# A transformer block's backward pass on one core: layer norm split over the first chunks, more buffers for the dK/dV stores, smaller loads in the first late stage

## The chip, the cores and the metric

The kernel runs on one core of a Trainium2 chip. The metric is the device time of one execution in microseconds (us), taken as the median of repeated runs. A core has TensorE (PE: matmuls; its weight loads, PEld, overlap them), VectorE (DVE), ScalarE (ACT), GpSimd (POOL) and SyncE (SP). In this kernel SP and POOL do little but issue DMAs, in the order in which the program gives them, and a DMA that has to wait holds up those behind it on the same queue. Matmul results lie in PSUM, everything else in SBUF or in the device's DRAM.

## The reference: what is computed

One block's output and the gradients of all inputs but one. x is 2048 x 576, there are 32 heads of width 128 with 2048 cached keys and values each, and the gated feed-forward part is 4608 wide; everything is bf16.

```python
xn = layernorm(x)
q = heads(xn @ wq); p = softmax(q @ k.T * 128 ** -0.5)
s = concat(p @ v) @ wo
h = sigmoid(xn @ w_gate) * (xn @ w_up)
out = x + s * silu(h @ w_down)
# returned: out, and by vjp(grad_out): dx, dk, dv, dwq, dwo, dw_gate, dw_up, dw_down
```

## The kernel before, in words

x is held as 16 row tiles of 128 rows (NT = 16). The work runs in stages.

**The first stage (L300 to L455)** loads x, `w_gate` and `w_up`, normalizes x, turns it (a transpose on PE through PSUM) into `xnT`, and computes the gate and up products. The 4608 columns are nine chunks of 512 in five groups: chunk 0 alone, then four groups of two (`groups1`). For every group, all row tiles are passed; for each chunk PE does five matmuls into `g_ps` (L418) and five into `u_ps` (L420), ACT takes the sigmoid (L425), DVE the product (L426), and POOL stores both (L439, L440). Both PSUM tiles have three buffers. The layer norm of a tile is: `bn` (statistics on DVE, L349 and L350), `rstd` for several tiles at once (a square root on ACT, L355, which needs another activation table than the sigmoid; then two short DVE operations), `norm` (ACT, L363), `turn` (five PE transposes, L369, into one of two `pt` buffers) and `put_T` (the copy into `xnT`, by the helper at L40). Tiles 0 and 1 are done first, tiles 2 and 3 and the statistics of tiles 4 to 6 ahead of the loop. All the rest is done within the 16 row tiles of chunk 0: the nine `bn` of tiles 7 to 15 in the first few, two or three per row, then one `rstd` for all nine; `norm` runs three tiles ahead of the row, `turn` two ahead. All weights are loaded through SP, after tiles 0 to 6 of x; tiles 7 to 15 follow the first chunk of both weights. From the second group on, a guard (`guard_step`) loads the key cache and `wq` in pieces through SP into the memory of x and sums their squares on ACT and DVE in turn, spread evenly over the chunk steps; before that, x is stored to DRAM (`xn_d`, L446).

**A second stage** (L503) computes the down product and the elementwise gradients.

**Attention (from L565)** is written as slots: a head has 32 slots, 16 for `main1` (scores by L600, exponentials by L618) and 16 for `main2` (`dp` by L670; then, for one half of the row, ACT L677 and DVE L678, and for the other DVE L673). Other work is put into slots by `plan`, with the slot number written out; b1 and b2 are a head's first slots of the two kinds. `main1` and `main2` send each row tile through a DMA transpose on SP (`PT`, `dST`, L594), and five slots later `tail1` and `tail2` (L647) multiply with it. dV and dK are summed in two halves of the query tiles (`Partial`): the first half goes to `part`, the second is added to it on DVE (L718) into a tile `kvo` and stored by POOL (L720), in four pieces of four blocks for each output. `kvo` comes from the pool `stg`, with two buffers. The second half of dV lies in slots b2 to b2+7, that of dK in b2+16 to b2+23, which are the next head's first slots. `scale_qn` (L636) scales a tile of Q for dK; `scale_don` does it for dV. The key and value loads of the next head (L178) are put into slots too.

**The late stages (from L825)**: the first one (L869 to L917) multiplies each row tile's attention output by `wo`. Its input `oT` is read from DRAM by a DMA transpose on SP (L554), two tiles ahead, into three places that attention has left (in `KQ`, `xnT` and `xn_all`). PE does 64 matmuls (L902) for a tile. DVE then needs `dsg`, `g2b` and `xb`, which `group_loads` loads through POOL (L876) for two tiles at a time, one group ahead, with two buffers; the output tile is stored from `xb` (L912). The next stages compute the weight gradients (L932, L985) and dx (L1103).

In the first late stage and after it, SP and POOL keep the order of the program, as they do in the first stage.

Of the kernel before, what the change touches and what calls it, by code (L numbers as in the profile page):

```python
# [9 lines left out]
bf = mybir.dt.bfloat16  # L10
f32 = mybir.dt.float32
PSUM = bass.MemoryType.PSUM
DRAM = bass.MemoryType.DRAM
P = 128
# [52 lines left out]
def kernel(  # L67
# [164 lines left out]
    with tc.tile_pool(name="pa", bufs=1) as pa:  # L232
# [75 lines left out]
        with tc.tile_pool(name="a1w", bufs=1) as wp:  # L308
# [5 lines left out]
                    for w_ in (wg_sb, wu_sb):  # L314
                        eng.memset(w_[:LO, DT - 1, c0:c1], 0.0)

            def load_w(w_, src, c0, c1):
                nf = DT - 1 if KPAD else DT
                if nf:
                    nc.sync.dma_start(w_[:, :nf, c0:c1], src[:nf * P, c0:c1].rearrange("(i p) c -> p i c", p=P))  # L320
                if KPAD:
                    nc.sync.dma_start(w_[LO:, nf, c0:c1], src[nf * P:, c0:c1])

            XF = min(7, NT)
            for xs, xe in ((0, 1), (1, 2), (2, XF)):
                if xs < xe:
                    nc.sync.dma_start(x_all[:, xs:xe, :], x2[xs * P:xe * P, :].rearrange("(t p) d -> p t d", p=P))
            zero_cols(nc.vector, 0, FCH)
            zero_cols(nc.gpsimd, FCH, F)
            for gi, (fa, fz) in enumerate(groups1):  # L330
                load_w(wg_sb, B_w_gate, fa * FCH, fz * FCH)
                load_w(wu_sb, B_w_up, fa * FCH, fz * FCH)
                if gi == 0 and NT > XF:
                    nc.sync.dma_start(x_all[:, XF:, :], x2[XF * P:, :].rearrange("(t p) d -> p t d", p=P))
            FMAX = nc.vector.BN_STATS_FMAX
            nchunk = 1
            while D % nchunk != 0 or D // nchunk > FMAX:
# [1 line left out]
            with tc.tile_pool(name="a0", bufs=3) as sb0, tc.tile_pool(name="a0ps", bufs=2, space=PSUM) as ps0, \  # L339
# [21 lines left out]
                def norm(st):  # L361
                    xt = x_all[:, st, :]
                    nc.scalar.activation(xt, xt, AF.Identity, bias=nbias[:, st:st + 1], scale=rstd_all[:, st:st + 1])  # L363

                def turn(st):
                    pts[st] = ps0.tile([P, 8, P], bf, name="pt", tag="tr")
                    for i in range(DT):
                        c0 = min(i * P, D - P)
                        nc.tensor.transpose(pts[st][:, i, :], x_all[:, st, c0:c0 + P], ident[:])  # L369

                def put_T(st, eng):
                    alt.copy(xnT[:, :, st * P:(st + 1) * P], pts.pop(st)[:, :DT, :], eng=eng)

                LA = min(2, NT)
                L1 = min(7, NT)
                for st in range(LA):
                    bn(st)
                rstd(0, LA)
# [4 lines left out]
                for a, b in ((LA, min(LA + 2, L1)), (min(LA + 2, L1), L1)):  # L383
# [4 lines left out]
                    if a == LA:  # L388
                        for st in range(a, b):
                            norm(st)  # L390
                bn_left = list(range(L1, NT))
                wd_left = list(range(0, FT, 3))

                def load_wd():
# [1 line left out]
                    f1 = min(f0 + 3, FT)  # L396
                    nc.gpsimd.dma_start(wd_sb[:, f0:f1, :], B_w_down[f0 * P:f1 * P, :].rearrange("(t p) d -> p t d", p=P))

                nstep = sum(NT * (fz - fa) for fa, fz in groups1[1:])
                ntot = len(pieces) + GLA  # L400
                step = 0
                for gi, (fa, fz) in enumerate(groups1):
                    for st in range(NT):
                        if gi == 0:
                            if LA + 2 <= st + LA + 1 < NT:
                                norm(st + LA + 1)
                            if st and st + LA < NT:
                                turn(st + LA)
                        srows = slice(st * P, (st + 1) * P)
                        a_row = rows.tile([P, NB2F * FCH], bf, name="a_row")  # L410
                        h_row = rows.tile([P, NB2F * FCH], bf, name="h_row")
                        for fc in range(fa, fz):
                            fs = slice(fc * FCH, (fc + 1) * FCH)
                            cs = slice((fc - fa) * FCH, (fc - fa + 1) * FCH)
                            g_ps = ps.tile([P, FCH], f32, name="g_ps")
                            u_ps = ps.tile([P, FCH], f32, name="u_ps")
                            for i, (d0, kd) in enumerate(dts):
                                nc.tensor.matmul(g_ps[:], lhsT=xnT[:, i, srows], rhs=wg_sb[:, i, fs], start=(i == 0), stop=(i == DT - 1))  # L418
                            for i, (d0, kd) in enumerate(dts):
                                nc.tensor.matmul(u_ps[:], lhsT=xnT[:, i, srows], rhs=wu_sb[:, i, fs], start=(i == 0), stop=(i == DT - 1))  # L420
                            if gi == 0 and st + LA < NT:
                                if st == 0:
                                    turn(LA)
                                put_T(st + LA, "s")
                            nc.scalar.activation(a_row[:, cs], g_ps[:], AF.Sigmoid)  # L425
                            nc.vector.tensor_tensor(h_row[:, cs], u_ps[:], a_row[:, cs], op=ALU.mult)  # L426
                            if gi:
                                step += 1
                                while gk[0] < min(ntot, ntot * step // max(1, nstep - 14)):
                                    guard_step()  # L430
                                    if gk[0] == ntot:
                                        guard_reduce()
                            elif bn_left:
                                for _ in range(min(3 if st == 0 else 2, len(bn_left))):
                                    bn(bn_left.pop(0))
                                if not bn_left:
                                    rstd(L1, NT)
                        nn = (fz - fa) * FCH
                        nc.gpsimd.dma_start(h_d[srows, fa * FCH:fz * FCH], h_row[:, :nn])  # L439
                        nc.gpsimd.dma_start(a_d[srows, fa * FCH:fz * FCH], a_row[:, :nn])  # L440
                        if gi > 1 and st % 2 and wd_left:
                            load_wd()
                    if gi == 0:
                        for t0 in range(0, NT, 4):
                            t1 = min(t0 + 4, NT)
                            nc.gpsimd.dma_start(xn_d[t0 * P:t1 * P, :].rearrange("(t p) d -> p t d", p=P), x_all[:, t0:t1, :])  # L446
                while gk[0] < ntot:
                    guard_step()
                    if gk[0] == ntot:
# [112 lines left out]
    def attention(fast):  # L562
        with ExitStack() as es:
# [126 lines left out]
            class Partial:  # L690
# [9 lines left out]
                def step(self):  # L700
                    kt = self.kt
                    j = kt % 4
                    if j == 0:
                        self.tile = acc_tile()
                    for qt in range(self.lo, self.hi):
                        nc.tensor.matmul(self.tile[:, j, :], lhsT=self.slabs[qt][:, kt * P:(kt + 1) * P], rhs=self.rhs[:, qt, :],  # L706
                                         start=(qt == self.lo), stop=(qt == self.hi - 1))
                    self.kt += 1
                    if j == 3 or self.kt == NT:
                        k0 = kt - j  # L710
                        if self.out_dram is None:
                            if self.factor == 1.0:
                                alt.copy(self.part[:, k0:kt + 1, :], self.tile[:, :j + 1, :], eng=self.eng)
                            else:
                                alt.scaled(self.part[:, k0:kt + 1, :], self.tile[:, :j + 1, :], self.factor, eng=self.eng)
                        else:
                            fo_ = stg.tile([P, 4, P], bf, name="kvo")
                            nc.vector.scalar_tensor_tensor(fo_[:, :j + 1, :], self.tile[:, :j + 1, :], self.factor, self.part[:, k0:kt + 1, :],  # L718
                                                           op0=ALU.mult, op1=ALU.add)
                            nc.gpsimd.dma_start(self.out_dram.rearrange("(p t) d -> p t d", t=NT)[:, k0:kt + 1, :], fo_[:, :j + 1, :])  # L720
# [30 lines left out]
            def plan(h):  # L751
# [22 lines left out]
                put(b1 + q(NSC + 2), NT * P, lambda: prep_vt(hd()))  # L774
                put(b1 + q(NTH + 2), NT * P, lambda: prep_qn(hd()))
                for qt in range(NT):
                    put(max(b1 + qt + 1, b1 + NT - 4 + qt // 2), 0, lambda qt=qt: scale_qn(hd(), qt))
                put(b2 + 1, 0, lambda: post1(hd()))
                parts = {}

# [54 lines left out]
    with late("pc") as pc, late("pcw") as pcw, late("pcf") as pcf, \  # L835
# [21 lines left out]
                if i == DT - 1 and KPAD:  # L857
                    nc.gpsimd.memset(wdT_sb[:LO, i, r0:r0 + WCH], 0.0)

        with late("c1l3", 2) as ldp3, late("c1s", 2) as sb, \  # L860
                late("c1ps", 2, space=PSUM) as ps, late("c1pt", 2, space=PSUM) as pst:
            wo_of = {}
            for view, h0, n, _ in wo_parts:
# [2 lines left out]
            oTs.append(oT_view(xn_all[:].rearrange("p t d -> p (t d)"), 0))  # L866
            if NT > 2:
                load_oT(oTs[2], 2)
            SG1 = ldiv(NT, 2)  # L869
            NG1 = NT // SG1  # L870

            def group_loads(g):
# [4 lines left out]
                    res.append(t_)  # L877
                return res

            groups = {0: group_loads(0)}  # L880
            pend_tr = []
            for st in range(NT):
                if st and st + 2 < NT:
                    load_oT(oTs[(st + 2) % 3], st + 2)
                g, sl = divmod(st, SG1)
                if sl == 0:
                    if g + 1 < NG1:
                        groups[g + 1] = group_loads(g + 1)
                    dsg, g2b, xb = groups.pop(g)
                if st >= NT - 2 - DT and len(wd_pieces) > (F // WCH - 1) * DT:  # L890
                    wd_piece()
# [285 lines left out]
```

## Time and profile before

| what | value |
|---|---|
| median of 14 runs | 5087.19 us (5064.58 to 5099.43) |
| the profiled execution's own time | 5106.43 us |
| its span, first to last instruction | 5104.4 us |
| mean granted clock of PE | 0.992 |
| PE busy, first stage's rows after chunk 0 (43 to 335.5 us) | 291.69 of 292.50 us |
| PE busy, start (8.87 to 43 us) | 27.43 of 34.13 us |
| PE busy, first tiles of the first late stage (3690 to 3728 us) | 22.18 of 38.00 us |
| PE busy, the rest of it (3728 to 3850 us) | 112.97 of 122.00 us |

How to read it: the profile is of one execution. A group's row gives the line, the engine, the operation, the tiles (out<-in), and then the busy time, the mean ns of one, and the idle time of the engine before it with what ended it. In the waits, "X <- Y: a, b, c" says that X's engine stood idle for Y, a us in total, b times, at most c us. In a timeline a row begins with start and duration in us, merges neighbours of one kind (x16), and ends with the idle time before it in brackets. The granted clock is the share of TensorE's full clock in a stretch. The DMA share is the mean busy share of the 16 DMA engines and can exceed 1 where packets overlap.

### The profile page before, as it was taken

How to read it: one execution, taken by the hardware profiler on the slowest of the kernel's cores; microseconds unless marked ns; L12 is line 12 of the kernel's file. 1: busy time of each engine (PE TensorE's matmuls, PEld its weight loads, DVE VectorE, ACT ScalarE, POOL GpSimd, SP SyncE). 2: the span in 40 equal slices, each digit the busy share in tenths (PEclk: the TensorE clock that was granted, in tenths of full speed). 3: DMA queues.
4: the chain of work that ended last, by engine and by line, in shares of the span. 5: the costliest groups of instructions: out<-in, count | busy, mean ns of one | idle time of the engine just before them, and what ended most of it. 6: DMA issues, size and time to landing. Idle time of an engine off the chain costs nothing.

```text
span 5104.4 us, 128938 instructions
## 1 busy us (share of the span) xinstructions
PE 4984.7 (98%) x54480; PEld 3486.7 (68%) x54480; DVE 2582.3 (51%) x6705; ACT 2574.9 (50%) x4636; POOL 938.9 (18%) x1449
## 2 busy tenths in 40 slices
PE   8999999999999999999999999999889999999999
PEld 4445777777777777777777777777645666555554
DVE  4544666666566666656656665666424444200111
ACT  5422666666666676666666666666413333211000
POOL 3322111111111111111111111111112222211000
PEclk9999999999999999999999999999999999999999
DMA  8777999999999999999999999999996665797986
GB/s 267 261 200 171 199 201 206 203 209 211 204 202 213 205 211 207 202 210 208 213 191 200 203 212 206 208 203 206 210 186 190 188 188 184 221 261 187 174 141 121
DMA packets 2762161, 1031.37 MB, mean 202 GB/s; under 512 B 2664737, under 2 KB 2668962, under 8 KB 2761570
## 3 DMA queue, kind: packets, MB, share of 16 engines
q1 hardware_dynamic: 2660354, 699.97, 74.9%
q0 software_dynamic: 101216, 323.05, 20.0%
q8 instruction: 428, 7.01, 0.6%
q14 instruction: 163, 1.34, 0.1%
HBM read 175.31 MB, written 182.13 MB: 70 GB/s over the span
## 4 chain that ended last, share of the span: by engine, by line
PE 85%; issue 7%; DMA 5%; DVE 2%; POOL 1%; ACT 1%; POOLq 0%; SPq 0%; DVEq 0%; ACTq 0%
PE acc L706 15%; PE acc L647 14%; PE acc L932 13%; PE sp L600 8%; PE acc L1103 7%; PE dp L670 7%; PE acc L213 5%; PE g_ps L418 3%; PE u_ps L420 3%; PE dh L985 3%; PE acc L503 2%; PE acct L146 2%; DMA out_dram<-kvo 2%; PE acc L902 2%; DMA KQ<-on_d 1%
## 5 line engine op out<-in xcount | busy, mean ns | idle before, releaser
L618 ACT ACTIVATE Pq<-sp 128x1024 bf16<-128x1024 f32 x1024 | 1047.0, 1023 | 319.6 <-PE sp L600 307.4
L706 PEld LDWEIGHTS <-Pq 128*128 128x128 bf16 x16384 | 1005.7, 98 | 242.9 <-issue 5.4
L677 ACT ACTIVATE t<-dp,negdelta 128x1024 bf16<-128x1024 f32 x512 | 571.1, 1116 | 222.7 <-PE dp L670 210.1
L673 DVE SCALAR_TENSOR_TENSOR Pq<-dp,negdelta,Pq 128x1024 bf16<-128x1024 f32 x512 | 655.1, 1279 | 43.8 <-PE dp L670 42.8
L670 PE MATMUL dp<-VT,dOT 128*128 128x512 bf16 x2048 | 614.4, 382 | 42.7 <-DVE Pq L673 42.7
L600 PE MATMUL sp<-KQ 128*128 128x512 bf16 x2048 | 609.9, 380 | 2.6 <-ACT Pq L618 2.4
L647 PEld LDWEIGHTS <-PT 128*128 128x128 bf16 x8192 | 502.6, 98 | 132.6 <-DMA PT<-Pq 11.9
L647 PE MATMUL acc<-Kn,dST 128*128 128x128 bf16 x8192 | 551.3, 219 | 6.5 <-DMA dST<-Pq 6.2
L647 PE MATMUL acc<-Vn,PT 128*128 128x128 bf16 x8192 | 547.8, 219 | 10.0 <-DMA PT<-Pq 9.9
L706 PE MATMUL acc<-dOn,Pq 128*128 128x128 bf16 x8192 | 547.0, 219 | 0.0
L706 PE MATMUL acc<-Qn,Pq 128*128 128x128 bf16 x8192 | 543.4, 220 | 0.0
L647 PEld LDWEIGHTS <-dST 128*128 128x128 bf16 x8192 | 491.9, 98 | 69.6 <-DMA dST<-Pq 8.8
L678 DVE TENSOR_TENSOR Pq<-t,Pq 128x1024 bf16<-128x1024 bf16 x512 | 354.2, 692 | 360.1 <-ACT t L677 353.4
L687 ACT ACTIVATE dq_n<-acc,rsc 128x128 bf16<-128x128 f32 x512 | 188.1, 367 | 340.3 <-PE acc L647 339.2
L1119 DVE SCALAR_TENSOR_TENSOR junk<-acc,xn_all 128x512 f32<-128x512 f32 (+1 forms) x32 | 13.9, 452 | 638.0 <-ACT dxn L1118 638.0
L720 POOL DMA_DIRECT2D out_dram<-kvo x256 | 140.3, 548 | 1067.5 <-DVE kvo L718 1067.5
L641 POOL DMA_DIRECT2D on_d<-o_n x128 | 97.0, 758 | 744.7 <-DVE junk L659 390.8
L987 DVE TENSOR_TENSOR du_blk<-dh,ah 128x256 bf16<-128x256 f32 x288 | 120.0, 417 | 194.5 <-PE dh L985 192.5
L718 DVE SCALAR_TENSOR_TENSOR kvo<-acc,part 128x512 bf16<-128x512 f32 x256 | 175.9, 687 | 78.4 <-DMA out_dram<-kvo 44.7
L670 PEld LDWEIGHTS <-dOT 128*128 128x128 bf16 x2048 | 164.1, 98 | 70.5 <-issue 48.3
L1118 ACT ACTIVATE dxn<-acc 128x512 f32<-128x512 f32 (+1 forms) x32 | 12.8, 406 | 394.9 <-PE acc L1103 387.4
L50 DVE TENSOR_SCALAR o_n<-acc,rinv_all 128x128 bf16<-128x128 f32 x352 | 123.2, 350 | 169.8 <-PE acc L647 169.8
(206 smaller groups left out, 6914.2 us busy)
## 6 DMA issues: line engine op xcount, KB each, us to landing
out_dram<-kvo POOLq DMA_DIRECT2D x256, 128.0 KB, 4.2
ah<-a_d POOLq DMA_DIRECT2D x18, 1024.0 KB, 7.1
ah<-h_d POOLq DMA_DIRECT2D x18, 1024.0 KB, 9.3
du_d<-du_blk POOLq DMA_DIRECT2D x18, 1024.0 KB, 8.0
dg_d<-dg_blk POOLq DMA_DIRECT2D x18, 1024.0 KB, 9.7
h_d<-h_row POOLq DMA_DIRECT2D x64, 256.0 KB, 3.4
x_all<-in_A_k_cache_dram SPq DMA_DIRECT2D x64, 256.0 KB, 3.9
a_d<-a_row POOLq DMA_DIRECT2D x64, 256.0 KB, 3.7
```

Source lines behind the costliest of these rows:

```text
L213: nc.tensor.matmul(av[:, :CH], lhsT=w[:, i, :], rhs=srcT[:, i, cs], start=(i == 0), stop=(i == DT - 1))
L600: nc.tensor.matmul(sp[:, c * CH:(c + 1) * CH], lhsT=hs.QT[:, qt * P:(qt + 1) * P], rhs=hs.KT[:, hf * HW_ + c * CH: hf * HW_ + (c + 1) * CH ...
L618: nc.scalar.activation(Pq[:, hsl], sp[:], AF.Exp, scale=SCALE, accum_out=hs.rsp[:, hf:hf + 1])
L647: nc.tensor.matmul(hs.acc[:, 0, :], lhsT=T[:, kt, :], rhs=rhs[:, kt, :], start=(kt == 0), stop=(kt == NT - 1))
L670: nc.tensor.matmul(dp[:, c * CH:(c + 1) * CH], lhsT=hs.dOT[:, qt * P:(qt + 1) * P], rhs=hs.VT[:, hf * HW_ + c * CH: hf * HW_ + (c + 1) * C ...
L673: nc.vector.scalar_tensor_tensor(Pq[:, hsl], dp[:], hs.negdelta[:, qt:qt + 1], Pq[:, hsl], op0=ALU.add, op1=ALU.mult)
L677: nc.scalar.activation(t[:], dp[:], AF.Identity, bias=hs.negdelta[:, qt:qt + 1], scale=1.0)
L678: nc.vector.tensor_tensor(Pq[:, hsl], t[:], Pq[:, hsl], op=ALU.mult)
L687: nc.scalar.activation(hs.dq_n[:, qt % G4, :], hs.acc[:, 0, :], AF.Copy, scale=hs.rsc[:, qt:qt + 1])
L706: nc.tensor.matmul(self.tile[:, j, :], lhsT=self.slabs[qt][:, kt * P:(kt + 1) * P], rhs=self.rhs[:, qt, :], start=(qt == self.lo), stop=(q ...
L932: nc.tensor.matmul(accs[j][:, :nn], lhsT=lhs[:, st, cols], rhs=rhs[:, st, n0:n0 + nn], start=(st == 0), stop=(st == NT - 1))
L1103: nc.tensor.matmul(self.accs[sl][j][:, :nn], lhsT=ch[:, kk, sl * P:(sl + 1) * P], rhs=wT[:, k0 + kk, n0:n0 + nn], start=(self.k + kk == 0) ...
```

## The change

Three parts.

1. *Attention.* `kvo` gets four buffers. `scale_qn` of tiles 8 to 15 moves from slots b2 to b2+3 (two per slot) to b2+8 to b2+15 (one per slot).
2. *First stage.* The order of loads becomes x tiles 0 and 1, gate chunk 0 (SP) and up chunk 0 (on ACT's queue), x tiles 2 to 6, x tiles 7 to 15, the other weights. The loop passes chunk 0 and the first group of two chunks for tiles 0 to 6, then both for tiles 7 to 15, then the other groups for all tiles. `norm` of tiles 4 to 6 is issued from the first row on; `bn` of tiles 7 to 15 one per chunk step while tiles 0 to 6 are at chunks 1 and 2, then `rstd` and one `norm` per step; a `turn` follows as soon as its `norm` has been issued. The `xn_d` stores and the guard's first steps come after the last of these.
3. *First late stage.* The loads are for one tile at a time, two tiles ahead, with four buffers; the output is stored tile by tile.

```diff
-            XF = min(7, NT)
-            for xs, xe in ((0, 1), (1, 2), (2, XF)):
...
+            for st in range(LA):
+                load_x(st, st + 1)
             zero_cols(nc.vector, 0, FCH)
             zero_cols(nc.gpsimd, FCH, F)
...
+            load_w(wg_sb, B_w_gate, 0, FCH)
+            load_w(wu_sb, B_w_up, 0, FCH, nc.scalar)
+            load_x(LA, L1)
+            load_x(L1, NT)
+            for fa, fz in groups1[1:]:
...
+                todo = {"norm": list(range(min(LA + 2, L1), L1)), "turn": list(range(LA, L1)), "bn": list(range(L1, NT))}
+
+                def ln_step(first):
+                    if first or not todo["bn"]:
+                        if todo["norm"]:
+                            norm(todo["norm"].pop(0))
+                        return
+                    bn(todo["bn"].pop(0))
+                    if not todo["bn"]:
+                        rstd(L1, NT)
+                        todo["norm"] = list(range(L1, NT))
+                        todo["turn"] = list(range(L1, NT))
+                        norm(todo["norm"].pop(0))
+
+                def turn_step():
+                    if todo["turn"] and not (todo["norm"] and todo["norm"][0] <= todo["turn"][0]):
+                        st = todo["turn"].pop(0)
+                        turn(st)
+                        return st
...
+                rows_order = [(gi, st) for half in ((0, L1), (L1, NT)) for gi in range(min(2, gi_max)) for st in range(*half)]
+                rows_order += [(gi, st) for gi in range(2, gi_max) for st in range(NT)]
...
+                        ready = None
+                        if n_row:
+                            ready = turn_step()
+                        if gi == 0 and st < L1 and todo["norm"]:
+                            ln_step(True)
...
+                        if not n_row:
+                            ready = turn_step()
+                        if ready is not None:
+                            put_T(ready, "s")
                         nc.scalar.activation(a_row[:, cs], g_ps[:], AF.Sigmoid)
                         nc.vector.tensor_tensor(h_row[:, cs], u_ps[:], a_row[:, cs], op=ALU.mult)
+                        if gi or st >= L1:
+                            if todo["bn"] or todo["norm"]:
+                                ln_step(False)
...
+                        if begin is not None:
+                            while gk[0] < min(ntot, ntot * (step - begin) // max(1, nsteps - 14 - begin)):
...
-                            fo_ = stg.tile([P, 4, P], bf, name="kvo")
+                            fo_ = stg.tile([P, 4, P], bf, name="kvo", bufs=4)
...
-                    put(max(b1 + qt + 1, b1 + NT - 4 + qt // 2), 0, lambda qt=qt: scale_qn(hd(), qt))
+                    put(max(b1 + qt + 1, b1 + NT - 4 + qt // 2 if qt < NTH else b1 + NT + qt), 0, lambda qt=qt: scale_qn(hd(), qt))
...
-        with late("c1l3", 2) as ldp3, late("c1s", 2) as sb, \
+        with late("c1l3", 4) as ldp3, late("c1s", 2) as sb, \
...
-            SG1 = ldiv(NT, 2)
+            SG1 = 1
...
-            groups = {0: group_loads(0)}
+            groups = {g: group_loads(g) for g in range(min(2, NG1))}
...
-                    if g + 1 < NG1:
-                        groups[g + 1] = group_loads(g + 1)
+                    if g + 2 < NG1:
+                        groups[g + 2] = group_loads(g + 2)
```

## The prediction

> **What bounds the kernel now.** I read the page first, then TensorE's waits, then the stretches where those waits lie.
>
> ```profile
> span 5104.4 us, 128938 instructions
> ...
> PE 4984.7 (98%) x54480; PEld 3486.7 (68%) x54480; DVE 2582.3 (51%) x6705; ACT 2574.9 (50%) x4636; POOL 938.9 (18%) x1449
> ```
>
> PE is busy 98%, so 5104.4 - 4984.7 = 119.7 us of idle time, and whatever PE does at less than full clock, is all that an edit off PE can win. The change takes no matmul away. TensorE's waits:
>
> ```profile
> PE dp L670 <- DVE Pq L673: 42.7, 46, 5.4
> PE acc L902 <- DMA KQ<-on_d: 24.4, 2, 16.7
> PE pt L369 <- ACT x_all L363: 13.3, 3, 6.6
> ```
>
> (us in total, times, longest.) Three causes, and each lies in one of the three places that the diff touches. First attention: one head, in the timeline.
>
> ```profile
> 2625.00 1.06 PE L706 MATMUL acc<-dOn,Pq 128*128 128x128 bf16 x16
> ...
> 2635.28 0.69 DVE L718 SCALAR_TENSOR_TENSOR kvo<-acc,part 128x512 bf16<-128x512 f32 x1 [5.59 <-DMA out_dram<-kvo]
> 2635.89 1.27 DVE L673 SCALAR_TENSOR_TENSOR Pq<-dp,negdelta,Pq 128x1024 bf16<-128x1024 f32 x1
> ...
> 2637.21 1.01 PE L670 MATMUL dp<-VT,dOT 128*128 128x512 bf16 x2 [3.97 <-DVE Pq L673]
> ...
> 2640.58 1.55 PE L706 MATMUL acc<-Qn,Pq 128*128 128x128 bf16 x16
> ```
>
> DVE stands 5.59 us before the fourth kvo, until the second one's store has landed; L673 is queued behind it and frees the PSUM of dp; PE waits 3.97 us. Afterwards the same sixteen matmuls take 1.55 us, not 1.06: the clock. Two stretches with their granted clock (PE busy, PEld, DVE, ACT, POOL, then clock, DMA share, GB/s):
>
> ```profile
> 2500.00:2600.00 100.00, 99.76 (x1295) 79.36 (x1293) 63.84 (x173) 68.61 (x117) 17.28 (x29) 1.00 1.10 207
> 2634.80:2641.60 6.80, 4.39 (x30) 3.27 (x30) 3.76 (x4) 2.49 (x3) 1.29 (x2) 0.50 1.23 198
> ```
>
> An undisturbed head leaves nothing to win (99.76 of 100; heads are 97.68 us apart there). Last, the start of the first late stage (issues and their time to landing), and the start of the kernel:
>
> ```profile
> dsg<-dsg_d POOLq DMA_DIRECT2D x3, 288.0 KB, 18.9
> ...
> KQ<-on_d SPq DMA_TRANSPOSE x1, 32.8
> ```
> ```profile
> 27.27 1.28 ACT L355 ACT_TABLE_LOAD   x1 [5.50 <-DVE mv_all L350]
> ...
> 30.28 0.71 PE L369 MATMUL pt<-ident,x_all 128*128 128x128 bf16 x5 [5.71 <-ACT x_all L363]
> ```
>
> **Part 1, four kvo buffers.** Removed: DVE's wait on kvo stores, 44.5 us in 16 waits in attention. Each output has four kvo (16 blocks by 4); the next output's follow eight slots later, above 20 us at 2.65 us a slot, and no kvo store took over 11.7 us to land, so four buffers never wait. On the path lies not 44.5 but PE's idle time behind it: the fifteen gaps above 0.3 us before L670 in attention sum to 35.3 us (0.4 to 5.4). After eight of them the clock falls to 0.50 for 3.4 or 6.8 us; half of the busy time in these windows (2.2 us of the 4.39 shown, 1.7 us in a short one) is lost: 2 x 2.2 + 6 x 1.7 = 15 us. Together 50 us.
>
> What is late next? The stores are slow because everything is: in this head the dST transposes issued at 2620.5 and 2623.7 took 11.6 and 12.1 us, against a median of 4.9. tail2 takes its dST five slots after the issue. I moved each tail2 start forward by its stall and set it against its landing: in 15 stalls the dST would be late in five, by 2.5, 0.3, 1.2, 0.2 and 0.3 us (one later one by 0.6): 5 us comes back. So -45 us; bounds -50 (no dST late) and -20 (the burst of transfers merely moves, and dST misses its slack as often as kvo does now).
>
> Moving eight scale_qn per head (L636, 0.246 us each): before, two per slot in slots b2 to b2+3, beside kvo, o_n and junk; now one per slot in b2+8 to b2+15, where DVE has 0.69 + 1.28 + 0.25 = 2.2 us for a slot of 2.65 us. Their reader, dK's second half, begins at b2+16. Hidden; cost 0, and at most 0.25 us a head (8 us) if L673 stood behind each without that slack; gain at most the same.
>
> **Part 2, the layer norm.** Removed: the gap of 5.71 us (all nine bn, 1.0 us each, then the square root with its table load, were due before the tenth tile) and its half clock: 27.0 to 33.8 at 0.50, PE busy 3.52 there, 1.8 us lost. Also the 0.99 us before tile 4's transpose, since norm(4) is now queued ahead of the first Sigmoid's table load. Sum 8.5 us. The nine bn, nine norm (0.86), nine copies (0.69) and the two table loads (1.28) move to chunk steps of 2.16 us, or 2.44 with a transpose: DVE 1.0 + 0.69, ACT 0.60 + 0.86 + 0.69 = 2.15. It fits, without slack on ACT, but PE has three PSUM buffers and turned tiles ahead, so the table loads hide. The xn_d stores (POOL) and the first guard loads (SP) move behind it; the guard's 91 steps then share some 100 chunk steps instead of 114, which ACT (44% busy there) and DVE (48%) take. SP issues the later weights ahead of them as before.
>
> Added: tiles 2 to 6 of x now follow both weight pieces. Before, x2-6 landed at 7.06, wg at 9.02, wu at 10.98. The bytes up to wu are the same, so x2-6 land near 10.9, wg at about 8.4. Before, 3.6 us passed from bn(2)'s start at 7.80 to norm(2)'s end at 11.4; begun at 10.9 it ends at 14.5. turn(2) waits for it behind a first row that now ends near 12.4: 2 us of idle PE. Behind it, ACT runs norm(4), which waits for bn(4..6), ahead of put_T(2) and the first Sigmoid; put_T(2) ends near 19.0, not 14.4, and row 2 starts near 19.3 instead of 17.4. Rows 3 and 4 wait for put_T and for the two buffers of pt. By these steps row 6 starts at about 29.6; it started at 34.7: gain 5. Bounds: +3 (a cold clock through these waits) and -10. I take -4.
>
> The Trainium skill ("DMA: Bandwidth & Descriptors", Rules for kernel authors) says that spreading DMAs over issuing engines brings no bandwidth, since all share the same DMA engines. The row agrees in its way: the DMA share is already 1.05 and more from 3 us on, one queue alone. So wu on ACT's queue gains SP's issue time only (0.66 + 0.77 us) and is paid by x2-6; without the rule I would have put turn(2) 2 us earlier.
>
> **Part 3, the late stage by tiles.** What could go: 16.66 us before the fourth tile's oT, with 2.5 us of half clock after it. Six group loads of 288 KB (1.77 MB) were issued within 4 us, oT's transpose at 3695.98 ran into them and landed after 32.8 us; in the undisturbed stretch an oT lands after 8.3. Now nine loads of 144 KB (1.33 MB) stand there, later three per tile. In the steady part a burst of three 288 KB loads and a store (1.18 MB) does not hold oT up, while 1.77 MB did: 1.33 is nearer to the first. Bounds: -19 and, below nothing, +10 (POOL stood 16.4 us before xb's load, until a store had landed; now nothing holds the loads back, and oT waits as long or longer). Between the ends I take -8. The gap of 7.8 us at 3829 follows from 2 MB of ah loads and wdT transposes: it stays. The last tile's three loads now queue behind the ah loads, +0 to +3 us; I take 0.
>
> Here a rule speaks against the change: the same page's rules advise coalescing into transfers of 1 MiB and more, and its section "Anatomy of one DMA" fits a DMA of POOL's kind with 2.0 us plus bytes / 436 GB/s. By it (an estimate) 24 loads of 288 KB cost 24 x 2.7 = 64 us, and 48 of 144 KB 48 x 2.3 = 112 us: +48 us if they ran singly. The rows: three such loads land 4 to 5 us after their issue, side by side, inside a tile's 8.1 us. POOL issues 24 loads and 8 stores more, 32 x 0.71 = 23 us over 16 tiles, and is mostly idle there. I follow the row: 0.
>
> **Sum.** -45 - 4 - 8 = -57 against the profiled execution's 5106.4 us: 5049. That execution lies 19 us above the median of 14 runs (5087.2); the runs themselves spread over 35 us, which fits stalls that come and go with DMA. If the 19 us were such stalls, the median has fewer to lose and the new median is near 5049; if they are the profiler's, it is 5087 - 57 = 5030. I take the middle: 5039.
>
> **Rivals.**
> A (likeliest, 0.60): as summed; 5012 to 5062.
> B (0.20): the DMA burst in each head stays, and dST waits take kvo's place: 20 us of the 50 are won, nothing in the late stage, 4 at the start: 5087 - 24 = 5063, range 5055 to 5077. For it: transfers take 11 to 12 us there whoever waits; against: dST's slack of five slots held in ten of 15 cases.
> C (0.06): late stage and start win in full (19 + 10) and kvo 50: 5087 - 79 = 5008.
> D (0.06): the x2-6 delay and the late stage's bound cost what kvo's lower bound wins: 5087 - 20 + 3 + 10 = 5080, no measurable change (within 0.2%, 10 us, is about what a measurement of this kernel cannot tell from none).
> E (0.08), slower: unblocked POOL keeps load bursts in flight beside every oT. A tile needs 1.05 MB of oT and 4 x 0.147 of loads and stores, 1.64 MB per 8.12 us, 202 GB/s; undisturbed the stage had 211, the disturbed stretch about 95. If the slow rate lasts, a tile takes 17 us, +9; from six tiles on it eats the 49 us of the other parts, over 13 tiles it is +117: 5087 - 49 + 117 = 5155. Against: before, the loads had the same mean rate, and twelve tiles ran undisturbed.
>
> Range 5010 to 5078. Faster 0.86, same 0.06, slower 0.08.
>
> **What will show it.** No wait of kvo on its store; L670's wait on L673 from 42.7 to below 10 us; clock 1.00 through most of attention; waits of L647 on dST up by some 5 us (B: 20 or more). No idle gap over 3 us at 24 to 31 us, but one of about 2 us before turn(2), and the Sigmoid's first table load later. KQ<-on_d at the late stage's start landing in under 20 us (E: several oT above 20). I am wrong if dST takes over kvo's waits, or if the oT gap stands as it was.

## The result, and the profile after

| | before | after | after / before |
|---|---|---|---|
| median, us | 5079.76 (47 runs, 5054.84 to 5101.96) | 5049.96 (10 runs, 5043.10 to 5058.41) | 0.994 (0.9926 to 0.9955) |
| profiled execution, us | 5106.43 | 5034.82 | 0.986 |

The change makes the kernel 0.6% faster, 30 us by the medians. The prediction was 5039 with a range of 5010 to 5078: the direction and the range held. (5039 was 48 us under the median of 5087.2 that stood at hand then.) The two profiled executions differ by more, 71.6 us: the one of before lies 27 us above its median, the one of after 15 us below. So a row by row comparison of these two profiles alone overstates the change by some 42 us, and the experiments have to show which of the differing rows belong to the change.

Lines have moved: up to 7 further at the start (turn L369 is L376, norm L363 is L370, `rstd` L355 is L362), 28 further from the chunk loop on (L670 is L698, L673 is L701, L718 is L746, L902 is L930).

The page's head for after (PE was 4984.7 of 5104.4 us before):

```profile
span 5033.0 us, 129057 instructions
...
PE 4966.5 (99%) x54480; PEld 3474.5 (69%) x54480; DVE 2580.9 (51%) x6705; ACT 2574.4 (51%) x4636; POOL 950.5 (19%) x1481
```

Idle time of PE fell from 119.7 to 66.5 us, and PE's own busy time by 18.2 us with the same 54480 matmuls: that fits half clock which is gone (mean granted clock 0.992 before, 0.997 after). The waits of PE in after (total us, times, longest):

```profile
PE pt L376 <- ACT x_all L370: 14.7, 10, 8.3
PE acc L675 <- DMA PT<-Pq: 11.4, 4, 5.9
PE dp L698 <- DVE Pq L701: 7.6, 32, 0.2
PE acc L930 <- DMA KQ<-on_d: 5.7, 2, 5.0
PE acc L675 <- DMA dST<-Pq: 3.5, 7, 1.0
```

Read against the three waits of before: `dp` on L673 fell from 42.7 to 7.6 us, and what is left is 32 waits of at most 0.2, one per head. The wait on `dST` did not grow (6.2 before, 3.5 after). The late stage's wait on `KQ` fell from 24.4 to 5.7. The layer norm's wait did not fall at all: 13.3 in three waits before, 14.7 in ten after (6.6 and 8.3 of it are the wait for the first tile).

DVE in one head of after, at the fourth `kvo` of an output, where before DVE stood 5.59 us:

```profile
2605.59 0.69 DVE L706 TENSOR_TENSOR Pq<-t,Pq 128x1024 bf16<-128x1024 bf16 x1 [0.76 <-ACT t L705]
2606.20 0.68 DVE L746 SCALAR_TENSOR_TENSOR kvo<-acc,part 128x512 bf16<-128x512 f32 x1
2606.80 1.27 DVE L701 SCALAR_TENSOR_TENSOR Pq<-dp,negdelta,Pq 128x1024 bf16<-128x1024 f32 x1
```

L746 follows its neighbour without a bracket, and so does L701. The stretch around it (us and busy time of PE, PEld, DVE, ACT, POOL, then clock, DMA share, GB/s):

```profile
2600.00:2700.00 100.00, 99.76 (x1294) 79.42 (x1293) 64.48 (x168) 67.87 (x115) 17.64 (x29) 1.00 1.09 207
```

99.76 of 100 us at full clock is what the prediction showed of an undisturbed head. In after almost all heads are such heads, 97.68 us apart; before, 13 of them were longer by more than 0.5 us, at most by 7.2 us.

At the late stage's start, the issues of after and their median us to landing (stretch 3633 to 3680):

```profile
dsg<-dsg_d POOLq DMA_DIRECT2D x6, 144.0 KB, 8.0
...
KQ<-on_d SPq DMA_TRANSPOSE x2, 21.2
```

Before, the transpose into `KQ` took 32.8 us; now the median of two is 21.2, and PE waits at most 5.0 us for `KQ` rather than 16.7. Whether the smaller loads did that, this pair can't say. The layer norm in after, where the second pass of tiles begins:

```profile
48.89 1.28 ACT L362 ACT_TABLE_LOAD   x1
...
52.81 0.45 PE L376 MATMUL pt<-ident,x_all 128*128 128x128 bf16 x5 [3.50 <-ACT x_all L370]
...
54.71 2.34 PE L448 MATMUL u_ps<-wu_sb,xnT 128*128 128x512 bf16 x5
...
59.96 0.45 PE L376 MATMUL pt<-ident,x_all 128*128 128x128 bf16 x5 [0.41 <-ACT x_all L370]
```

The gap of 5.71 us has become one of 3.50 us at tile 7, with half clock behind it (L448's five matmuls take 2.34 us here and 1.24 at full clock), and then seven gaps of 0.36 to 0.41 us, one for each of tiles 9 to 15.

### The profile page after: what moved, and what is told of

It reads as the page before. It is cut to its first block, busy times and chain, and to the rows that moved or that the text cites. A ratio compares the mean times of both kernels' runs of the same rounds, so it can differ in the third digit from the quotient of the medians.

```text
span 5033.0 us, 129057 instructions
## 1 busy us (share of the span) xinstructions
PE 4966.5 (99%) x54480; PEld 3474.5 (69%) x54480; DVE 2580.9 (51%) x6705; ACT 2574.4 (51%) x4636; POOL 950.5 (19%) x1481
## 4 chain that ended last, share of the span: by engine, by line
PE 90%; DMA 3%; issue 3%; DVE 2%; ACT 1%; POOL 0%; POOLq 0%; SPq 0%; ACTq 0%; DVEq 0%
PE acc L734 17%; PE acc L675 16%; PE acc L960 13%; PE sp L628 9%; PE dp L698 8%; PE acc L1131 7%; PE acc L213 5%; PE g_ps L446 3%; PE u_ps L448 3%; PE dh L1013 3%; PE acc L531 2%; PE acct L146 2%; PE acc L930 2%; DMA dST<-Pq 1%; DMA KQ<-on_d 1%
## 5 line engine op out<-in xcount | busy, mean ns | idle before, releaser
L701 DVE SCALAR_TENSOR_TENSOR Pq<-dp,negdelta,Pq 128x1024 bf16<-128x1024 f32 x512 | 655.0, 1279 | 37.6 <-PE dp L698 37.6
L698 PE MATMUL dp<-VT,dOT 128*128 128x512 bf16 x2048 | 609.9, 379 | 7.6 <-DVE Pq L701 7.6
L675 PEld LDWEIGHTS <-PT 128*128 128x128 bf16 x8192 | 502.4, 98 | 134.3 <-DMA PT<-Pq 13.3
L675 PEld LDWEIGHTS <-dST 128*128 128x128 bf16 x8192 | 492.0, 98 | 66.5 <-DMA dST<-Pq 5.6
L633 DVE TENSOR_REDUCE rs_all<-rsp 128x1 f32<-128x2 f32 x512 | 78.0, 152 | 256.4 <-ACT Pq L646 254.2
L646 ACT ACTIVATION_READ_ACCUMULATOR Pq<-sp 128x1 f32 x1024 | 200.4, 196 | 0.0
```

What stands on the lines that cost most here:

```text
L646: nc.scalar.activation(Pq[:, hsl], sp[:], AF.Exp, scale=SCALE, accum_out=hs.rsp[:, hf:hf + 1])
L675: nc.tensor.matmul(hs.acc[:, 0, :], lhsT=T[:, kt, :], rhs=rhs[:, kt, :], start=(kt == 0), stop=(kt == NT - 1))
L698: nc.tensor.matmul(dp[:, c * CH:(c + 1) * CH], lhsT=hs.dOT[:, qt * P:(qt + 1) * P], rhs=hs.VT[:, hf * HW_ + c * CH: hf * HW_ + (c + 1) * C ...
L701: nc.vector.scalar_tensor_tensor(Pq[:, hsl], dp[:], hs.negdelta[:, qt:qt + 1], Pq[:, hsl], op0=ALU.add, op1=ALU.mult)
```

## The experiments

Two theories for the gain. Theory K: it is all the `kvo` store; the layer norm and the late stage give about nothing, and what the first pair shows in the late stage is chance. Theory S: the three parts each give what the first pair of profiles shows, some 50, -2.5 and 20 us. Below, "stage 2" is the time at which the first matmul of the second stage begins, "attention" goes from the first scores matmul (`sp`, 151.9 us later in every profile) to the late stage's first `oT` matmul, "late" from there to the next stage's first matmul (in us, of each profile). For orientation, the first pair of profiles: before 335.6, 3200.5, 158.3; after 338.2, 3148.6, 137.6.

### Each part alone

**The kernel before, unchanged, beside the others.**

> The kernel before, unchanged, for a second profile. Theory (the profiled execution of before had more stalls than a usual one, its time was 26 us above the median): kvo waits of DVE in sum 20 to 40 us instead of 44.7, in other heads than before, a time of 5065 to 5090 us. Rival (the profiler itself adds the 26 us): again 5100 to 5110 us with kvo waits of about 45 us in the same heads.

Measured (a single run): 5073.62 us; stage 2 at 335.1, attention 3190.9, late 133.2. Its waits of DVE on the store and of PE on L673 and on `KQ`:

```profile
DVE kvo L718 <- DMA out_dram<-kvo: 37.9, 15, 5.3
```
```profile
PE dp L670 <- DVE Pq L673: 38.5, 46, 4.3
...
PE acc L902 <- DMA KQ<-on_d: 1.8, 1, 1.8
```

The store's waits are there again, 37.9 us of them, and, against the expectation, in the same groups of heads (listed below at the ring of eight); the late gap isn't: 1.8 us with nothing changed. The issues at that place (3670 to 3715) show why it could be:

```profile
dsg<-dsg_d POOLq DMA_DIRECT2D x3, 288.0 KB, 4.7
...
KQ<-on_d SPq DMA_TRANSPOSE x2, 13.0
```

With the old loads of 288 KB the transposes landed after 13.0 us (median) in this execution. So the 16.7 us on `KQ` do not come in every execution.

**Part 1 alone.**

```diff
-                            fo_ = stg.tile([P, 4, P], bf, name="kvo")
+                            fo_ = stg.tile([P, 4, P], bf, name="kvo", bufs=4)
```

> The kernel before with four kvo buffers and nothing else. Theory (the stores' wait is the main gain): no wait of kvo on its store, TensorE's wait for L673 under 10 us (42.7 before), heads 97.7 us apart almost throughout, and the largest share of the change's 30 us in the medians: 18 to 30 us faster than the kernel before. Rival B (dST waits take its place): kvo's wait gone but under 10 us gained, TensorE's wait for dST up from 6 to 20 us or more. The start (5.7 us gap) and the late stage (gaps of about 17 and 8 us) stay as before.

Measured: 5042.61 against 5082.07 us, ratio 0.9922 (0.9898 to 0.9947), -39.5 us, more than the 18 to 30 expected. Attention 3156.3, of which 12.9 us is one wait on `PT` in the last head. PE's waits:

```profile
PE dp L670 <- DVE Pq L673: 7.8, 32, 0.4
...
PE acc L647 <- DMA dST<-Pq: 2.8, 4, 1.5
```

The wait of `kvo` on its store is gone, and that on L673 is where after has it. This one keyword gives at least the gain measured for the whole change; the direct comparison follows below. (`scale_qn` stands here in its old slots; the heads are 97.68 us apart all the same, so its move gives nothing that these profiles show.)

**Part 3 alone** (four buffers, `SG1 = 1`, two tiles ahead; the rest as before).

> The kernel before with the first late stage's loads tile by tile and nothing else. Theory: the third part's 21 us in the profiled pair is partly chance; in the medians 3 to 15 us faster, the gap before the fourth tile under 10 us, attention as before with its kvo waits (30 to 50 us). Rival (chance only: a transfer burst is as likely to hold oT up as before): within 3 us of the kernel before, a gap above 10 us before some oT. Rival E: slower, several oT landing after more than 20 us.

Measured: 5080.3 against 5082.07 us, ratio 1.0001 (0.9985 to 1.0017; the quotient of these two medians is 0.9997, inside the interval). Late 139.0, PE's wait on `KQ` 5.9 us, `kvo` 36.4 us. The 3 to 15 us that were expected did not show: no gain or loss can be told, and one of up to some 8 us either way isn't excluded. Over the eleven profiles with the old loads, the late stage took 131.8 to 158.3 us (median 139.7); in the three with the new ones 137.6, 139.0 and 140.4. Four of the eleven have one wait of 13.4 to 17.2 us on `KQ` (the first profile of before, part 2 alone, and two kernels with the lagged layer norm below), and late stages of 150.7 to 158.3 us; with the new loads the longest such wait is 7.1 us. The new loads may guard against this; three profiles can't show that, and neither can they show whether the new first stage, which three of the four have and one of the other seven, makes it likelier.

**Part 2 alone** (the new first stage; the rest as before).

> The kernel before with the layer norm part alone (order of rows, order of the first loads, up weights on ACT's queue). Theory from the profiled pair: the first stage ends 2 to 4 us later than before, since one gap of 5.7 us gives way to one of 3.5 us and seven of 0.4 us, and the first matmul begins 0.7 us later: 1 to 4 us slower. My prediction's step: 4 us faster. A measurement of 5 rounds may not tell the two apart; the time of the first matmul of the second stage in the trace does (334.7 us before, 337.4 us after the whole change).

Measured: 5077.75 against 5082.07 us, ratio 0.9992 (0.9978 to 1.0006). The interval doesn't tell -4 from +2 us. The trace does: stage 2 begins at 338.5, as in after (338.2) and in a second profile of it (338.6), while the profiles with the old first stage have 335.1 to 336.8. So this part costs about 2.5 us of the first stage, less than the times can tell. The turns of tiles 7, 8 and 9 in this kernel:

```profile
53.37 0.45 PE L376 MATMUL pt<-ident,x_all 128*128 128x128 bf16 x5 [3.50 <-ACT x_all L370]
...
57.27 0.45 PE L376 MATMUL pt<-ident,x_all 128*128 128x128 bf16 x5 [1.29 <-ACT x_all L370]
...
60.29 0.45 PE L376 MATMUL pt<-ident,x_all 128*128 128x128 bf16 x5 [0.41 <-ACT x_all L370]
```

The gap before tile 7's turn is the same 3.50 us, but here the clock stayed at 1.00 (53.4 to 56.8 us), and PE waited 1.29 us more at tile 8 instead. From tile 7's turn to tile 9's it took 6.92 us, against 7.15 in after with its half clock: ACT sets the pace here, and the half clock itself cost about 0.2 us.

### What the layer norm lost

**A tile's turn one step later than its norm.**

```diff
-                    if todo["turn"] and not (todo["norm"] and todo["norm"][0] <= todo["turn"][0]):
+                    if todo["turn"] and not (todo["norm"] and todo["norm"][0] <= todo["turn"][0] + (todo["turn"][0] >= L1)):
```

> The layer norm part alone, with one edit: for tiles 7 to 15 a turn is issued one chunk step later, when the next tile's norm has been issued too. Theory (in the change the turn follows its norm without slack, so TensorE waits for the square root's table load and for each norm): the gap of 3.5 us with its half clock and the seven of 0.4 us go, the first stage's last row ends 6 to 8 us earlier than with the layer norm part as it is (338.5 us until the second stage's first matmul, so 331 to 333). Rival (ScalarE's order is the limit: norm, copy and sigmoid take 2.15 us of a 2.44 us step): the gaps come back at the copies into xnT, 336 or more.

Measured (a single run, 5068.79 us): stage 2 at 330.8, 7.7 us before part 2 alone. Of the nine gaps at the turns of tiles 7 to 15 in part 2 alone (7.5 us together) one is left, 1.34 us before tile 7's.

**The same, with the old order of loads** (up chunk 0 on SP, tiles 2 to 6 ahead of the weights).

```diff
+            load_x(LA, L1)
...
-            load_w(wu_sb, B_w_up, 0, FCH, nc.scalar)
-            load_x(LA, L1)
+            load_w(wu_sb, B_w_up, 0, FCH)
```

> As the one before, and x tiles 2 to 6 are loaded ahead of the weights again, all on SP's queue. Theory (the new order of loads delays the first statistics and the first matmul): the first matmul starts 0.7 to 1.5 us earlier than 9.6 to 9.9 us, and the second stage 1 to 2 us earlier than in the run with the late turn alone. Rival (the new order helps the first row): the second stage starts no earlier.

Measured (a single run, 5078.85 us): stage 2 at 329.0, another 1.8 us earlier. But not by the path expected: the first product began at 9.48 us, against 9.57 with the new order. What went are the four gaps before the turns of tiles 2 to 5, 1.9 us in the kernel with the lag alone and none here. The table load and the turns in this kernel:

```profile
47.19 1.28 ACT L362 ACT_TABLE_LOAD   x1
...
51.11 0.45 PE L376 MATMUL pt<-ident,x_all 128*128 128x128 bf16 x5 [1.34 <-ACT x_all L370]
...
53.77 0.45 PE L376 MATMUL pt<-ident,x_all 128*128 128x128 bf16 x5
```

Same table load, but the gap is 1.34 us instead of 3.50, and tile 8's turn has no bracket: its norm is one step old. After 1.34 us the clock stayed at 1.00 (51.0 to 57.8).

### Why the stores are slow, and how many buffers it takes

**Without the value loads** of heads 1 to 31, which then use head 0's values.

```diff
-                        put(pl + q(skew + 3 + c), 0, lambda c=c: load_v(hd(), c, 4))
+                        pass
```

> The kernel before without the loads of the value cache for heads 1 to 31 (all heads use head 0's values), to see what makes the kvo stores slow. Theory V (four loads of 128 KB meet the dST transposes and the stores within 3 us, and all of them slow down): the longest kvo landing in a head falls from 8 to 12 us to under 6 in most heads, kvo waits of DVE under 8 us in sum instead of 38 to 45, TensorE's wait for L673 near 8 us. Rival R (the buffers of the transposes decide, since slow heads come back every seven heads): the waits stay above 25 us in the same heads, 1 to 2, 7 to 9, 14 to 16, 21 to 23, 28 to 30.

Measured (a single run): 5029.75 us with two `kvo` buffers; attention 3151.4; all heads 97.68 us apart. DVE's wait on the store:

```profile
DVE kvo L718 <- DMA out_dram<-kvo: 2.8, 3, 2.2
```

Four loads of 128 KB per head, put into the slots where dV's four pieces are stored, are what makes those stores late: without them the longest of dV's four stores in a head takes 4.3 to 6.0 us (9.8 in the last head), with them 4.7 to 11.7, and two buffers are nearly enough. dK's stores, which have no value loads beside them, did not get shorter (longest of a head 4.0 to 8.3 us with the value loads, 4.4 to 8.6 without), which speaks against the smaller traffic as a whole being the reason. Whether the same loads in other slots would do no harm was not tried. The issues of kernel `kvo4` (2580 to 2680) show these loads where they are, and their price:

```profile
out_dram<-kvo POOLq DMA_DIRECT2D x8, 128.0 KB, 3.9
...
Vn<-in_A_v_cache_dram POOLq DMA_DIRECT2D x4, 128.0 KB, 9.2
...
dST<-Pq SPq DMA_TRANSPOSE x16, 5.6
```

and without them (2600 to 2700):

```profile
out_dram<-kvo POOLq DMA_DIRECT2D x9, 128.0 KB, 4.0
...
dST<-Pq SPq DMA_TRANSPOSE x18, 4.6
```

The medians hardly move; it is the few transfers in the burst that take twice and three times as long.

**A ring of eight `PT`/`dST` tiles.** In both profiles of before the longer heads lie in the groups 1 and 2, 7 to 9, 14 to 16, 21 to 23 and 28 to 30 (one or another head of a group is missing each time): a group every seven heads. The pool of these tiles has seven buffers.

```diff
-            wpt = pool("wpt", 7 if fast else 4)
+            wpt = pool("wpt", 8 if fast else 4)
```

> The kernel before with eight instead of seven buffers for PT and dST, nothing else. Slow heads came back every seven heads in all profiles; 32 transposes per head on a ring of seven repeat every seven heads, on a ring of eight every head. Theory R (the place in the ring decides which heads are slow): the groups seven heads apart vanish, the heads are all alike, all slow or none. Rival V (only the V loads count, and the seven is by chance or from elsewhere): three to four slow heads in every seven as before, kvo waits 35 to 45 us in sum.

Measured (a single run, 5080.14 us): the heads of the same groups are long, and `kvo` waits 34.1 us. The ring isn't the reason; why the groups come every seven heads stays open.

### The parts together, side by side

**The changed kernel again, part 1 again, three buffers instead of four, and part 1 with the lagged layer norm**, all against the same runs of before (5085.81 us).

```diff
-                            fo_ = stg.tile([P, 4, P], bf, name="kvo")
+                            fo_ = stg.tile([P, 4, P], bf, name="kvo", bufs=3)
```

> The whole change once more, on the same chip as the next three. Theory (kvo alone carries the gain, the layer norm part costs 2 to 3 us, the late stage nothing): 28 to 40 us faster than the kernel before, 0 to 8 us slower than four kvo buffers alone. Rival (the parts add as the first profiled pair showed): 60 us or more faster, and faster than four buffers alone by 15 us or more.

> Four kvo buffers alone, beside the whole change on the same chip. Theory: 32 to 42 us faster than the kernel before, the same as or up to 8 us faster than the whole change. Rival: slower than the whole change by 15 us or more.

> Three kvo buffers, nothing else. Theory (only the fourth kvo of an output waits, for the second store; with three it waits for the first, which is issued five us earlier and ahead of the V loads): the wait is gone or under 5 us in sum, and the time within 5 us of that of four buffers. Rival (each buffer takes off a part): kvo waits of 10 to 20 us in sum, and 10 to 20 us slower than four.

> Four kvo buffers and the layer norm part with the late turn and the old order of loads; the late stage and the Q scaling as before. Theory: the first stage ends 6 to 7 us before that of the kernel before, so 38 to 48 us faster than the kernel before and 8 to 14 us faster than the whole change: the fastest of all. Rival (what is won at the start is lost to chance at the late stage): within 4 us of four kvo buffers alone.

| kernel | median us | ratio to before (95%) | stage 2 | attention | late |
|---|---|---|---|---|---|
| the whole change | 5042.10 | 0.9927 (0.9904 to 0.9949) | 338.6 | 3148.3 | 140.4 |
| part 1 alone, again | 5042.68 | 0.9927 (0.9902 to 0.9952) | 335.4 | 3153.0 | 139.1 |
| three `kvo` buffers alone | 5042.29 | 0.9921 (0.9898 to 0.9945) | 335.2 | 3149.9 | 138.0 |
| part 1 and the lagged layer norm, old loads | 5036.02 | 0.9911 (0.9889 to 0.9934) | 329.1 | 3148.1 | 156.3 |

The first three can't be told apart: part 1 is the change's gain, and the third buffer is all of part 1. In the profile with three buffers L718 has no wait on the store at all. With two, it is always the fourth `kvo` of dV that waits, for the second one's store (all 17 waits in the first profile of before, all 15 in the second); with three it would wait for the first one's, which is issued earlier and ahead of the value loads. The last kernel has the lowest median, 6 us under the whole change; 8 to 14 us were expected, and the intervals overlap, so the times don't prove it faster than the changed kernel. Its stage 2 begins 9.5 us earlier in the trace. Its own profile also has the long wait in the late stage:

```profile
PE acc L930 <- DMA KQ<-on_d: 18.9, 2, 13.4
```

which is one of the four in eleven named above.

## Why the prediction was right, and where it was wrong

**Part 1, -45 us: right in mechanism and size.** Timed alone it is -39.5 and -43.1 us, which are medians against medians; in the traces, attention fell from 3191 (the second profile of before) or 3200 (the first) to 3156 and 3153 with this part alone, -35 to -47, and to 3149 and 3148 in the whole change. Both terms of the step are there with their sizes: in the first pair of profiles PE's idle time in attention fell from 64.2 to 27.8 us, by 36.4 (35.3 reckoned), and its busy time, with the same matmuls, from 3136.3 to 3120.8 us, by 15.5 (15 reckoned for the half clock). The 5 us that dST was to give back did not come: the burst of transfers stayed (in after the longest `dST` landing of a head still reaches 11.6 us), but the wait on `dST` is 2.8 to 7.3 us in the six profiles with three or four buffers, and 2.4 to 6.2 in the seven with two and all the loads. The five slots of slack held, so rival B fell. That four buffers suffice was right; that three do was not seen.

**`scale_qn`, 0:** nothing in the profiles speaks against it.

**Part 2, -4 us: the sign was wrong.** The step that failed reads "PE has three PSUM buffers and turned tiles ahead, so the table loads hide". There are no turned tiles ahead. `turn_step` issues a tile's turn as soon as the next tile's norm stands first in the list, that is one chunk step after its own norm, and ACT had gone through the table load, the square root and the norm in one piece. So PE waited 3.50 us at tile 7, spent 1.6 us more on the next two products at half clock (3.74 us instead of 2.16; where the clock stayed full it waited 1.29 us at tile 8 instead), and then 2.7 us in seven gaps, since norm, copy and sigmoid need nearly all of a step on ACT, as the same sentence had said ("without slack on ACT"). The order of loads had a second error. The 2 us wait before `turn(2)` did not come: `bn(2)` began at 9.49 us, not 10.9, PE did not stand before that turn at all (13.28 us in the rows below), and row 6 began at 27.57, 2 us before the 29.6 reckoned. (The DMA share, read as 1.05 and more from 3 us on, was 0.83 and 0.72 from 3 to 4 us and 1.04 or more only from there.) What the step did not have is that the start came late (rows of after's first 50 us, DVE and PE):

```profile
5.56 0.82 DVE L356 BATCH_NORM_STATS2 stats<-x_all 128x6 f32<-128x288 bf16 x2 [1.03 <-DMA x_all<-in_A_x_dram]
...
9.61 2.32 PE L446 MATMUL g_ps<-wg_sb,xnT 128*128 128x512 bf16 x5
...
13.28 0.44 PE L376 MATMUL pt<-ident,x_all 128*128 128x128 bf16 x5
```

Tile 1's statistics begin at 5.56 us instead of 3.95: the tile landed at 5.54 instead of 3.49, with the up weights, issued on ACT's queue at the same time, in flight beside it (they landed at 5.75; that they are the reason was not tried alone). The first product begins at 9.61 instead of 8.87 (8.1 to 9.7 over the profiles with the old order, 9.6 to 9.9 with the new, so at most a small loss). The terms that I can name, 0.7 at the start, 1.6 in three gaps before row 4, 3.5, 1.6 and 2.7, make 10.1 us against the 8.5 removed: +1.6 of the +2.7 by which stage 2 is later in the pair; 1 us stays unassigned, and the terms are not independent: an earlier first product can be lost again in the gaps behind it (part 1 with the lagged layer norm began at 8.14 us, had two gaps of 0.68 and 0.65 us, and reached stage 2 at 329.1; the same first stage alone began at 9.48, had none, and reached it at 329.0). The run with the lagged turn shows the turn to be the cause: with one step more between norm and turn, 7.7 us are won.

**Part 3, -8 us: not shown, and its premise failed.** "What could go" was read from one profile, and the 16.66 us are not in every execution: with nothing changed the next profile had 1.8 us there, and such a wait is in four of eleven. Timed alone the part is 1.0001, so -8 lies at the edge of what that run excludes. The other half of that step held: 48 loads of half the size cost nothing that can be told, as the row had it and not the fixed price of each transfer (the prediction's estimate of +48 us would be a ratio of 1.009; the interval ends at 1.0017). The sign named for this part, `KQ` landing in under 20 us, was missed by little (a median of 21.2 of two in after). Rival E fell: the late stage took 137.6 us in after.

**The sum, 5039.** The prediction left open whether the profile's excess over the median was stalls or the profiler's. The second profile of before answers that: it had fewer stalls (37.9 us of `kvo` waits instead of 44.7; 133 us in the late stage instead of 158) and was 33 us faster. So the excess was stalls (25 of the 33 us lie in the late stage, 10 in attention), of the kind that the sum was removing, and "near 5049" was the right branch: 5049.96 was measured. By the medians of the later runs of after (5042.1) the truth is between the branches. That the sum of the terms was so near is partly luck: -45 was right, -4 and -8 were not.

## What to carry to other kernels

Before a stall is priced from one profile, ask whether it is in a second: the store's wait came back in every profile with two buffers and the value loads, the late stage's long gap in four of eleven, and only the first edit showed in the times. A wait on a store's buffer is bought off with the smallest ring in which the waiting write falls on a store that has already landed; here that was one buffer more, and two more gave the same. A half clock behind a gap is not a cost of its own where another engine sets the pace: the same 3.50 us gap, once with and once without it, led to the same place within 0.2 us. When work is spread over steps, look at the distance in steps between the maker and the taker of each tile: moved work that fits an engine's busy time still stalls the next engine if its result is wanted one step later.

## What the runs showed of the hardware

At the late stage's bad start the DMA share was 1.21 while only 95 GB/s moved (3700 to 3722 us of the first profile), against 207 GB/s at a share of 1.10 in an undisturbed head. Ordinary DMAs on POOL's queue and DMA transposes on SP's were in flight together in both; what makes the bad stretch so slow stays open. In attention, taking four 128 KB loads out of a head brought the longest of dV's four stores from up to 11.7 us to at most 6.0 (heads 0 to 30).

Gaps from about 2 us on can cost clock, but a gap's length alone does not tell. After the gap of 2.10 us at 2043.6 in the first profile of before, PE was fully busy at a granted clock of 0.59 for 3.4 us; after the 3.50 us in after's first stage it was 0.62, and after the same 3.50 us with part 2 alone 1.00. Over all fourteen profiles (from 40 us on, with full clock before the gap), PE's gaps of 1 to 2 us had half clock beginning within them or within 3.5 us behind them in 2 of 65 cases, gaps of 2 to 3 us in 33 of 67, and longer ones in 72 of 77. What decides among the gaps of equal length was not tried.
